# A fused convolution and hard-swish feed-forward kernel: one PSUM tile per output round, a plain first block, weight rounding in two steps

**Chip, cores, metric.** One core of one Trainium2 chip. The metric is the device time of one execution in microseconds (us), the median of several runs.

## The reference

```python
# attention part: causal depthwise convolution of 7 taps, softmax weights per head
w = softmax(weight)                                  # (8 heads, 7)
y[b,s,d] = sum_k w[head(d), k] * x_pad[b, s+k, d]    # x: (8, 4096, 192) fp32
# feed-forward part on the 32768 rows of y
h = y @ w_in                                         # (32768, 192) x (192, 2048)
g = h * clip(h + 3, 0, 6) / 6
out = g @ w_out                                      # (32768, 2048) x (2048, 192)
```

The feed-forward weights arrive as 64-bit floats and are rounded to fp32 on the chip, by integer and fp32 operations on their two halves. Everything else is fp32.

## The kernel before

It works on 32 blocks of 1024 rows. A block has an **h phase** (16 units: six fp32 matmuls, two row tiles side by side, then a Relu on ScalarE and the product g on VectorE) and an **out phase**. The out phase uses Strassen's seven products of half-size matrices in place of eight; they run four side by side in column tiles of 32, in five full rounds and one short one. The sums S1 to S4 of g are made on VectorE.

```python
ps = ctx.enter_context(tc.tile_pool(name="ps", bufs=4, space=bass.MemoryType.PSUM))

def banks():
    return ps.tile([P, 2, N], F32, name="banks")     # two halves, meant as one PSUM bank each; 4 such tiles

def out_phase(i, conv):
    ba, bb, bc = banks(), banks(), banks()
    b = [t[:, k] for t in (ba, bb, bc) for k in range(2)]     # six rounds, three tiles
    def three(k, n, n4, q4):                                  # one full round into b[k]
        side_by_side(*[out_mm(b[k], q, n, q, every) for q in range(NQ)],
                     out_mm(b[k], NQ, n4, q4, every))
    ...
    three(0, 1, 2, 0)
    nc.scalar.copy(out=p1[:], in_=b[0][m])
    piece(p2, 0, b[0], NQ)                                    # also a ScalarE copy
    three(1, 5, 2, 1)
    piece(p2, 1, b[1], NQ)
    for u in conv:                                            # 7 taps of the next block's y
        u()
    three(2, 7, 2, 2)
    ...
```

In block 0 the weights are rounded between the matmuls. One unit (1/8 of `w_in` or of `w_out`) is a chain over three engines:

```python
def to_f32(dst, st):
    low, high = st[:, :, 0], st[:, :, 1]
    nc.scalar.mul(rest, low, 2.0**-52)
    nc.vector.tensor_scalar(scale, high, 0x7FF00000, op0=bitwise_and)
    nc.gpsimd.tensor_scalar(scale, scale, (1023-127) << 20, 0.0, subtract, max)   # L142
    nc.gpsimd.tensor_scalar(scale, scale, 255 << 20, 8.0, min, mult)              # L146
    nc.vector.tensor_scalar(top, high, 0xFFFFF, 0x100000, bitwise_and, bitwise_or)
    nc.vector.scalar_tensor_tensor(sig, top, 2.0**-20, rest, mult, add)
    nc.vector.scalar_tensor_tensor(scale, high, 0x80000000, scale, bitwise_and, bitwise_or)
    nc.gpsimd.tensor_tensor(dst, sig, scale, mult)                                # L161
...
for p in range(NP):                       # NP = 8
    if i == 0:
        ... load two units ahead ...
        if p + 1 < NP: w_in_unit(p + 1)   # rounding, then two swap copies by DMA
    h_unit(i, p); h_unit(i, NP + p)
    if p % 2: s_unit(p - 1)
if i == 0:
    for j in range(NP): w_out_unit(j)     # all of w_out, after the h phase of block 0
out_phase(i, conv_units(i + 1))
```

(Operand names shortened, cuts marked with dots.)

## Time and profile before

| | before |
|---|---|
| median (range) | 2746.17 us (2746.01 to 2746.58, 3 runs) |
| span of the profiled run | 2742.7 us |
| TensorE / VectorE / ScalarE / GpSimd busy | 92 / 72 / 26 / 3% |
| mean granted clock of TensorE | 0.983 |
| block 1 begins | 203.5 us |
| period of blocks 1 to 31 | 81.65 us |

The names of lines in the profile of before: L240 h matmuls, L271 out matmuls, L245 Relu, L246 g, L258 sums, L295 and L319 ScalarE copies of a round, L300 VectorE adds, L211 taps. "banks<-y,w_in" reads "writes tile banks from y and w_in"; each fp32 matmul appears as two records.

### The profile page before, as it was taken

The numbers are of one execution on the slowest core, as the hardware profiler recorded it, in microseconds if no ns is written. First come the engines' busy times: TensorE is split into PE (matmuls) and PEld (weight loads), VectorE is DVE, ScalarE is ACT, GpSimd is POOL, SyncE is SP. The second block draws the span as 40 slices with busy tenths as digits, with TensorE's granted clock in tenths as the row PEclk, the third lists the DMA queues.
The fourth block names the chain that finished last, engine by engine and source line by source line (L and its number), as shares of the span: only waits on it lengthen the run. The fifth ranks groups of instructions, "written<-read, shape, count | busy, mean of one in ns | idle before, by whom it ended". The sixth has DMA issues, their size and how long they took to land.

```text
span 2742.7 us, 37945 instructions
## 1 busy us (share of the span) xinstructions
PE 2530.7 (92%) x16896; PEld 933.7 (34%) x16896; DVE 1969.1 (72%) x1775; ACT 710.2 (26%) x754; POOL 81.6 (3%) x84
## 2 busy tenths in 40 slices
PE   5469999999999999999999999999999999999998
PEld 2113333333333333333333333333333333333332
DVE  5547867777867777877777877777786777786775
ACT  2102322222322222332222332222232222232221
POOL 2440000000000000000000000000000000000000
PEclk9679999999999999999999999999999999999999
DMA  3100111100111100111110011110011110011100
GB/s 78 49 21 18 21 24 24 24 10 18 21 24 24 24 13 15 20 24 24 24 24 7 19 23 24 24 24 10 18 21 24 24 24 10 18 21 24 24 13 12
DMA packets 223156, 60.91 MB, mean 22 GB/s; under 512 B 204560, under 2 KB 210704, under 8 KB 222992
## 3 DMA queue, kind: packets, MB, share of 16 engines
q1 hardware_dynamic: 217344, 52.19, 10.3%
q10 hardware_dynamic: 5648, 6.30, 0.9%
q8 instruction: 132, 2.16, 0.3%
q14 instruction: 32, 0.26, 0.0%
HBM read 31.72 MB, written 25.17 MB: 21 GB/s over the span
## 4 chain that ended last, share of the span: by engine, by line
PE 91%; ACT 3%; DVE 3%; POOL 2%; issue 1%; DMA 0%; ACTq 0%; DVEq 0%
PE banks L240 48%; PE banks L271 43%; ACT c L295 2%; DVE c L300 1%; POOL scale L146 1%; POOL scale L142 1%; ACT c L319 1%; POOL w_out L173 0%; DVE y L211 0%; DVE s L258 0%; POOL w_out L161 0%; DVE scale L157 0%; DVE g L246 0%; DMA stage<-in_moe_w_in_dram 0%; DVE g L258 0%
## 5 line engine op out<-in xcount | busy, mean ns | idle before, releaser
L240 PE MATMUL banks<-y,w_in 64*128 64x512 f32 x6144 | 1345.2, 594 | 47.9 <-DVE y L211 26.4
L271 PE MATMUL banks<-g,w_out 128*32 128x512 f32 x6144 | 1188.6, 598 | 91.4 <-POOL w_out L161 46.0
L240 PEld LDWEIGHTS banks<-y,w_in 64*128 64x128 f32 x6144 | 597.8, 188 | 794.8 <-issue 750.3
L245 ACT ACTIVATE r<-banks,half 128x1024 f32<-128x1024 f32 x512 | 570.5, 1114 | 822.2 <-PE banks L240 613.6
L246 DVE SCALAR_TENSOR_TENSOR g<-r,banks 128x1024 f32<-128x1024 f32 x512 | 615.7, 1218 | 201.4 <-ACT r L245 190.1
L271 PE MATMUL banks<-s,w_out 128*32 128x512 f32 x4608 | 673.4, 594 | 64.6 <-ACT c L295 64.6
L271 PEld LDWEIGHTS banks<-g,w_out 128*32 128x32 f32 x6144 | 306.6, 110 | 459.2 <-issue 302.3
L300 DVE TENSOR_TENSOR c<-c,banks 96x512 f32<-96x512 f32 (+1 forms) x256 | 172.5, 684 | 377.5 <-ACT c L295 373.1
L271 PEld LDWEIGHTS banks<-s,w_out 128*32 128x32 f32 x4608 | 183.5, 110 | 546.0 <-issue 413.5
L295 ACT COPY c<-banks 32x512 f32<-32x512 f32 x192 | 111.1, 579 | 952.8 <-PE banks L271 952.4
L211 DVE SCALAR_TENSOR_TENSOR y<-x,c_sb,y 128x1536 f32<-128x1536 f32 x192 | 349.3, 1819 | 6.8
L258 DVE TENSOR_TENSOR g<-g 128x1024 f32<-128x1024 f32 x128 | 156.9, 1226 | 4.4
L258 DVE TENSOR_TENSOR s<-g 128x1024 f32<-128x1024 f32 x128 | 156.9, 1226 | 4.4
L258 DVE TENSOR_TENSOR s<-g,s 128x1024 f32<-128x1024 f32 x128 | 156.8, 1225 | 4.4
L258 DVE TENSOR_TENSOR s<-s,g 128x1024 f32<-128x1024 f32 x128 | 155.9, 1218 | 0.0
L300 DVE TENSOR_TENSOR c<-c,c 96x512 f32<-96x512 f32 x64 | 44.0, 687 | 107.2 <-ACT c L295 106.1
L305 DVE STREAM_TRANSPOSE xt<-c 96x512 f32<-96x512 f32 x128 | 90.6, 708 | 4.4
L319 ACT COPY c<-banks 96x512 f32<-96x512 f32 x32 | 18.6, 582 | 203.6 <-PE banks L271 203.6
L207 DVE TENSOR_SCALAR y<-x,c_sb 128x1536 f32<-128x1536 f32 x32 | 57.8, 1805 | 0.0
L157 DVE SCALAR_TENSOR_TENSOR scale<-stage,scale 128x384 uint32<-128x384 uint32 x16 | 8.9, 559 | 48.7 <-POOL scale L146 48.7
L142 POOL TENSOR_SCALAR scale<-scale 128x384 uint32<-128x384 uint32 x16 | 24.4, 1524 | 76.3 <-DVE scale L138 76.3
L146 POOL TENSOR_SCALAR scale<-scale 128x384 uint32<-128x384 uint32 x16 | 24.0, 1503 | 1.3
(21 smaller groups left out, 72.2 us busy)
## 6 DMA issues: line engine op xcount, KB each, us to landing
out_dram<-xt SPq DMA_DIRECT2D x384, 64.0 KB, 2.0
x<-in_x_dram SPq DMA_DIRECT2D x56, 388.5 KB, 5.7
x<-in_x_dram SPq DMA_DIRECT2D x8, 384.0 KB, 4.8
stage<-in_moe_w_in_dram ACTq DMA_DIRECT2D x16, 192.0 KB, 3.5
stage<-in_moe_w_out_dram ACTq DMA_DIRECT2D x8, 384.0 KB, 3.1
w_in<-w_in SPq DMA_DIRECT2D x16, 96.0 KB, 2.2
w_sb<-in_weight_dram ACTq DMA_DIRECT2D x2, 1.8 KB
```

Of the source, the lines that this page charges most:

```text
L142: nc.gpsimd.tensor_scalar(out=scale[:], in0=scale[:], scalar1=float((1023 - 127) << 20), scalar2=0.0, op0=ALU.subtract, op1=ALU.max,)
L146: nc.gpsimd.tensor_scalar(out=scale[:], in0=scale[:], scalar1=float(255 << 20), scalar2=8.0, op0=ALU.min, op1=ALU.mult,)
L207: nc.vector.tensor_scalar(out=y[:], in0=x[:, :, 0:N], scalar1=c, scalar2=None, op0=ALU.mult)
L211: nc.vector.scalar_tensor_tensor(out=y[:], in0=x[:, :, k : k + N], scalar=c, in1=y[:], op0=ALU.mult, op1=ALU.add,)
L240: nc.tensor.matmul(out=h[:, k], lhsT=w_in[r, slots[k], s, :], rhs=y[r, s, :], start=(s == 0), stop=(s == K3 - 1),)
L245: nc.scalar.activation(r6[:], h[:], ACT.Relu, bias=half[:], scale=1.0 / 6.0)
L246: nc.vector.scalar_tensor_tensor(out=g[:, c % NP, c // NP], in0=r6[:], scalar=1.0, in1=h[:], op0=ALU.min, op1=ALU.mult,)
L258: nc.vector.tensor_tensor(out=o[:, r], in0=x[:, r], in1=y[:, r], op=op)
L271: lambda p=p: nc.tensor.matmul(out=bank[j * QS : (j + 1) * QS], lhsT=w_out[:, p, w, cols], rhs=x[:, p], start=(p == ks[0]), stop=(p == ks[ ...
L295: nc.scalar.copy(out=dst[q * QS : (q + 1) * QS], in_=src[j * QS : (j + 1) * QS])
L300: nc.vector.tensor_tensor(out=out, in0=x, in1=y, op=op)
L305: nc.vector.transpose(out=xt[:], in_=c)
```

## The change

The intent: (1) every out round takes a tile of its own, so that TensorE never waits for the evacuation of a neighbour; for that the order of the products becomes 1, 4, a short 2, 7, 6, 3, and S2 and S4 are made late in wide instructions. (2) Block 0 needs no sums: it multiplies plain g, eight half products. (3) Rounding of weights is cut in a first and a second step, one unit begun ahead; the clamp moves from GpSimd to ScalarE. (4) All loads are issued up front; the first convolution goes in thirds, so that the first four h units can begin with the first third of y.

```diff
-    stg = ... bufs=3;  cnv = ... bufs=2
+    stg = ... bufs=2 * NP;  cnv = ... bufs=3
...
+        def first(self):
+            nc.vector.tensor_scalar(scale, high, 0x7FF00000, bitwise_and)
+            nc.vector.tensor_scalar(top, high, 0xFFFFF, 0x100000, bitwise_and, bitwise_or)
+            nc.scalar.activation(over, scale, Relu, bias=bias_e[:, 0:1], scale=-1.0)
+            nc.scalar.activation(scale, over, Relu, bias=bias_e[:, 1:2], scale=-8.0)
+            nc.scalar.mul(rest, low, 2.0**-52)
+        def second(self):
+            nc.vector.scalar_tensor_tensor(scale, high, 0x80000000, scale, ...)
+            nc.vector.scalar_tensor_tensor(sig, top, 2.0**-20, rest, mult, add)
+            nc.gpsimd.tensor_tensor(dst, sig, scale, mult)
+            self.then()                                   # w_in: the two swap copies
...
+    w_in_st = [load_w_in(nc.scalar if j < 2 else nc.sync, j) for j in range(NP)]
+    w_out_st = [load_w_out(nc.sync, j) for j in range(NP)]
...
-        ba, bb, bc = banks(), banks(), banks()
-        b = [t[:, k] for t in (ba, bb, bc) for k in range(2)]
+        def three(n, n4, q4):
+            bank = banks()[:, 0]
...
+    def out_direct(i, work):                              # block 0: plain products
+        parts = [(k, q) for k in range(G) for q in range(G * NQ)]
+        for r in range(0, len(parts), 4):
+            bank = banks()[:, 0]
+            ... four column tiles x 16 matmuls, transpose from PSUM, store ...
...
+        begin(); begin(); ... next(ended).second(); next(ended).second()
+        conv0 = conv_units(0, [slice(s, s + 1) for s in range(K3)])
+        for s in range(K3):
+            for u in conv0[s * KC : (s + 1) * KC]: u()
+            advance(1) if s else begin()
+        early = [(c, banks()) for p in range(2) for c in (p, NP + p)]
+        for s in range(K3):
+            for c, h in early: h_mm(0, c, h, s)
+        for n, (c, h) in enumerate(early):
+            h_out(c, h)                                   # Relu, g
+            if n: advance(1)                              # begin a unit, end one
+        for p in range(2, NP):
+            h_unit(0, p); advance(1)
+            h_unit(0, NP + p)
+            if p < 5: advance(1)
+        out_direct(0, conv_units(1, [slice(0, K3)]))
```

## The prediction

> **What bounds the kernel now.** I read the page first (busy shares, the 40 slices), then the chain that ended last over one block in the middle, then the waits of TensorE in two stretches (0 to 204 us and from 200 us on), then the chain and the windows of the start.
>
> From the page: TensorE is the busy engine, but its first slices are poor, at a low granted clock.
>
> ```profile
> PE 2530.7 (92%) x16896; PEld 933.7 (34%) x16896; DVE 1969.1 (72%) x1775; ACT 710.2 (26%) x754; POOL 81.6 (3%) x84
> ...
> PE   5469999999999999999999999999999999999998
> ...
> PEclk9679999999999999999999999999999999999999
> ```
>
> A slice is 68.6 us. So the kernel has two regimes: a start of some 200 us, and 31 equal blocks. One block of the second regime, from the chain (start us, length us, what):
>
> ```profile
> 203.61 41.40 PE banks L240 x192
> 245.01 7.08 PE banks L271 x64
> ...
> 252.11 0.58 ACT c L319
> ...
> 252.71 0.59 ACT c L295
> ...
> 253.34 13.98 PE banks L271 x128
> ...
> 267.35 0.59 ACT c L295
> ...
> 267.98 13.98 PE banks L271 x128
> ...
> 281.99 0.59 ACT c L295
> ...
> 282.60 0.69 DVE c L300
> ...
> 283.33 1.92 PE banks L271 x16
> 285.26 1.05 PE banks L240 x3
> ```
>
> The period is 285.26 - 203.61 = 81.65 us, and in it TensorE stops three times for an evacuation: after out rounds 1, 3 and 5, never after 2 and 4. Rounds 1 and 2 write the two halves of one tile (`ba`), 3 and 4 of `bb`, 5 and 6 of `bc`: the second half waits until the readers of the first half are through, although it writes other addresses. The waits of TensorE from 200 us on say the same in total (us, times, longest):
>
> ```profile
> PE banks L271 <- ACT c L295: 62.5, 62, 1.3
> PE banks L271 <- DVE c L300: 45.4, 32, 1.4
> ```
>
> That is 107.9 us over 31 blocks, 3.48 us in each. The same question for 0 to 204 us gives the start's own waits; its two largest:
>
> ```profile
> PE banks L271 <- POOL w_out L161: 46.0, 8, 12.6
> PE banks L240 <- DVE y L211: 26.4, 1, 26.4
> ```
>
> TensorE waits for the rounding of the weights: the chain of the start has two GpSimd steps of 1.5 us per unit (L142, L146), 16 units one after the other, the last eight of them in out round 1 of block 0 (matmuls at 120.03, 126.75, 133.48 ..., every 6.7 us). Block 1 begins at 203.5 us.
>
> **What the Trainium skill says.** (1) "Perfetto Trace Analysis", section "Matmuls": independent matmul groups should rotate through different PSUM banks, so that the evacuation of one lies beside the matmuls of the next. The trace agrees: the three waits stand exactly where two rounds share a tile. (2) "TensorE: Matmul & The Clock Gate", section "Wait — 56ns, not 53.3ns?": a warm pass of N columns starts every N / 2.4 GHz + about 2.5 ns, so 512 columns take 215.8 ns, and at half clock twice the column time. Here a fp32 pair (two row tiles) or quad (four column tiles) starts every 0.431 us, two such passes; the first ones after the start stand 0.85 us apart, from 26.44 to 29.87 us. (3) "DMA: Bandwidth & Descriptors", section "Queues, rings and completion order": each issuing engine has one ring per DMA engine, consumed in ring order. No run here shows a long backlog: the swap copies of `w_in` land in 2.2 us (median) because little stands before them. (4) "PSUM — Partial Sum Buffer", section "Engine vs sequencer instructions": ScalarE and VectorE are strict FIFO; in the trace, too, their instructions run in program order.
>
> **Part 1: one tile per out round.** A block has 96 pairs in the h phase (192 records / 2) and 84 half-passes in quads: 10,752 out records / 32 blocks / 4. That is 180 starts; at 0.4315 us (41.41 us / 96 from first h start to first out start) they take 77.7 us. The new order has just as many: five rounds of 128 records and a short one of 16. So each block can lose 81.65 - 77.7 = 3.95 us: the 3.48 us of waits and three drains of the array of about 0.17 us that then lie under the next round. Times 31: 122 us.
>
> Does a new wait come? With four tiles, each request waits for the readers of the one four before it. Let T be the end of the h phase. VectorE: last g at T+2.4; S1, S3 of the last pair until T+4.9; the four wide sums S2, S4 (2048 columns, estimated 2.3 us from 1.22 us per 1024) until T+14.1; four taps of 1.85 us until T+21.5; the short round's adds and one store until T+25; three taps until T+30.6; then the adds of rounds 7 and 6. TensorE's rounds end at T+6.9, 13.8, 15.5, 22.4, 29.3, 36.2. S2 is needed at T+22.4, S4 at T+29.3, y at T+36.2 (slack 5.6 us). The next block's first four h units take the tiles of the short round (free at T+25), of 7 and of 6 (T+33), and of 3 (T+38, needed at T+44). Nothing waits. VectorE in total per block: 16 g (19.5) + 16 half sums (19.0) + taps (12.9) + 10 adds and 4 transposes (9.7) = 61 of 77.7 us; not the bound.
>
> **Part 2: block 0 with plain products.** It removes the S sums (16 x 1.22 = 19.6 us of VectorE) from the start and costs TensorE 12 outputs x 16 steps / 4 side by side x 2 = 96 starts instead of 84: 41.4 us instead of 36.2, so +5.2 us.
>
> **Part 3: rounding in two steps, clamp on ScalarE.** GpSimd loses 2 x 1.5 us per unit and keeps the product (1.0 us); VectorE keeps 0.35 + 0.35 + 0.56 + 0.61, with issue 1.95 us; ScalarE goes from one instruction of 0.55 us to three, 1.65 us. One unit is begun ahead of the one that is ended. But the order is strict: g of unit n, then the bit operation of a new unit on VectorE, then three ScalarE instructions, and only behind these the Relu of h unit n+1, on which the next g waits. One round trip: 1.22 + 0.35 + 0.08 + 1.75 + 1.11 + 0.04 = 4.5 us, against 2.58 us of TensorE for an h unit. Eleven such trips lie in block 0: 50 us.
>
> **Part 4: conv by thirds and loads up front.** Stage 0 lands at 9.3 us as now. VectorE: bit operations, c_sb, both second steps until about 14.3, then three thirds of 7 x 0.67 us with a rounding between: 19, 24.5, 31.3 us. TensorE could start at 19 us. But the swap copies, without which no h unit is complete, go to the SP ring behind the loads that were issued before them. All loads are 7.1 MB; from 2 to 10 us the queues moved 198 GB/s, with some 225 at the plateau, so they end at 2.2 + 31.5 = about 33.5 us, and the first swap lands then. So thirds gain nothing. Four early units: 24 pairs with a cold beginning; the first is through at 43.3, its Relu at 44.4. g0, g1 until 47; ten round trips and g11 until about 92.5; this frees the tile of the last h unit, which ends at 96 to 97 (clock 0.8 as now in that stretch). Then 41.4 us of direct rounds, with the last rounding, the last g (102 us) and conv 1 (13 us) beside them: **block 1 begins at about 137 us**, against 203.5. If the swaps land early, at about 128.
>
> **The sum.** 136 (between the two, nearer the first) + 31 x 77.7 = 2408.7, + tail. The tail is now 2742.7 - (203.5 + 31 x 81.65) = 8.1 us: a copy, three small adds, an add, a transpose (4.1 us), stores. New: three adds and two transposes (3.6 us), so 7.6. Span 2552. The runs stand 3.5 us above the span of the profile now (2746.2 against 2742.7): **2556 us**, ratio 0.931.
>
> **The rivals.** (a) A new wait in each block, because y, S2 or a tile comes late: VectorE has 5.6 us of slack ahead of the h phase; 1 us of wait in each block makes +31 us, 2587. For it: VectorE is in order and its queue is full from T to T+33. Against: 61 of 77.7 us. (b) The start gains what its author wants: no backlog, TensorE from 19 us on, ScalarE and VectorE not in each other's way (3.2 us per unit, the VectorE sum): block 1 at 115, 2535 us. (c) The start gains little: loads slower than now, half clock through block 0 (5.15 us per h unit): block 1 at 155, 2575 us. (d) The waits within a tile were only the cover of another limit, such as the weight loads of the column tiles: then 81.65 stays, and the time is 2675. Against: after rounds 2 and 4 nothing waits now, and starts stay 0.43 us apart.
>
> **Range and chances.** The 31 blocks are sure to about +0.5 us each (+15 us, hardly anything below), the start to about -18 and +15. So 2536 to 2580. Faster by over 2% (under 2691) even where (a) or (c) comes true: 0.98.
>
> **What will show it.** The period of a block, first h matmul to first h matmul, should be 77.7 us, with no wait of TensorE on an evacuation; a period of 78.5 or more means (a), 81.6 means (d). The first h matmul at 33 us shows the backlog, at 19 us none. Gaps between successive g of 4.5 us show the round trip, 3.2 us rival (b). The end of block 0 should stand at 128 to 140 us, and GpSimd should be busy for about 16 + 7 us. I am wrong if the block period misses 77.7 by over 0.5 us or block 1 begins outside 115 to 155.

## The result, and the profile after

| | before | after |
|---|---|---|
| median (range) | 2746.09 us (2744.26 to 2746.58, 4 runs) | 2548.68 us (2548.14 to 2549.26, 4 runs) |
| span of the profiled run | 2742.7 us | 2547.2 us |
| block 1 begins | 203.5 us | 133.6 us |
| period of blocks 1 to 31 | 81.65 us | 77.59 us |
| from the last block's end to the end | 8.1 us | 8.3 us |
| mean granted clock | 0.983 | 0.999 |

The ratio is 0.9282, 95% interval 0.9266 to 0.9298. A ratio here is the mean time of one kernel's fast runs over that of the other's in the same rounds, so not quite the ratio of the medians.

The page of after, busy time and two of the rows of 40 slices:

```profile
PE 2495.4 (98%) x16944; PEld 945.9 (37%) x16944; DVE 1923.2 (76%) x1640; ACT 740.9 (29%) x810; POOL 28.6 (1%) x24
...
PE   4899999999999999999999999999999999999998
...
PEclk9999999999999999999999999999999999999999
```

The poor first slices have shrunk from three to two, and the clock is full almost everywhere. (Before 36.9 us the trace of after holds no clock record, which the page counts as full clock; the weight loads of successive pairs stand 0.85 us apart there from 33.1 to 36.5 us, against 0.43 later.) Line numbers have moved: L254 h matmuls, L281 out matmuls, L262 Relu, L263 g, L231 taps of y, L184 and L185 the swap copies, L158, L161 and L164 the rounding on ScalarE, L148 the first bit operation, L347 and L364 (L365 in one run) ScalarE copies of a round. The chain over one block in the middle (start us, length us, what):

```profile
873.30 36.19 PE banks L281 x336
909.49 41.40 PE banks L254 x192
950.89 9.13 PE banks L281 x81
```

Where before had three copies and an add between pieces of out rounds, the out phase is one piece of 336 records, and the period is 950.89 - 873.30 = 77.59 us. All of TensorE's waits in the whole run (us, times, longest) are now these three, and all lie before 92 us:

```profile
PE banks L254 <- DVE y L231: 23.7, 1, 23.7
PE banks L254 <- DVE g L263: 13.3, 9, 1.6
PE banks L254 <- DMA w_in<-w_in: 6.4, 1, 6.4
```

From the chain of the start:

```profile
17.33 6.57 DMA stage<-in_moe_w_out_dram
...
23.98 8.09 DMA w_in<-w_in
...
32.12 10.39 PE banks L254 x35
...
92.27 41.34 PE banks L281 x384
```

The first h matmuls that matter start at 32.12 us, when the first swap copy has landed; the plain out phase of block 0 runs from 92.27 to 133.60 us. Between, the chain goes round a loop over two engines, once per h unit:

```profile
57.81 0.04 DVE g L263
...
58.95 0.36 DVE scale L148
...
59.34 0.63 ACT over L158
...
60.05 0.62 ACT scale L161
...
60.66 0.45 ACT rest L164
...
61.12 1.01 ACT r L262
...
62.15 0.06 DVE g L263
```

From g to g it takes 62.15 - 57.81 = 4.34 us, and the Relu (ACT r, L262) stands behind three rounding instructions, which wait for VectorE's bit operation, which waits in VectorE's order for the g before.

So the saving of 195.5 us in span is 31 x 4.06 = 125.9 us in the blocks and 69.9 us in the start, minus 0.2 at the end.

### The profile page after: what moved, and what is told of

The parts are those of the page before. It is cut to its first block, busy times and chain, and to the rows that moved or that the text cites. A ratio compares the mean times of both kernels' runs of the same rounds, so it can differ in the third digit from the quotient of the medians.

```text
span 2547.2 us, 37923 instructions
## 1 busy us (share of the span) xinstructions
PE 2495.4 (98%) x16944; PEld 945.9 (37%) x16944; DVE 1923.2 (76%) x1640; ACT 740.9 (29%) x810; POOL 28.6 (1%) x24
## 4 chain that ended last, share of the span: by engine, by line
PE 97%; ACT 1%; DMA 1%; issue 1%; DVE 0%; ACTq 0%; SPq 0%; DVEq 0%
PE banks L254 51%; PE banks L281 46%; ACT r L262 0%; DMA stage<-in_moe_w_in_dram 0%; DMA w_in<-w_in 0%; DMA stage<-in_moe_w_out_dram 0%; ACT over L158 0%; ACT rest L164 0%; ACT scale L161 0%; DVE g L263 0%; DVE scale L148 0%; SPq L112 0%; DVE c L352 0%; ACTq L112 0%; ACTq L85 0%
## 5 line engine op out<-in xcount | busy, mean ns | idle before, releaser
L254 PE MATMUL banks<-y,w_in 64*128 64x512 f32 x6144 | 1334.4, 591 | 43.4 <-DVE y L231 23.7
L263 DVE SCALAR_TENSOR_TENSOR g<-r,banks 128x1024 f32<-128x1024 f32 x512 | 623.3, 1218 | 428.6 <-ACT r L262 428.6
L254 PEld LDWEIGHTS banks<-y,w_in 64*128 64x128 f32 x6144 | 598.1, 187 | 779.2 <-issue 751.7
L262 ACT ACTIVATE r<-banks,half 128x1024 f32<-128x1024 f32 x512 | 569.9, 1114 | 789.5 <-PE banks L254 723.8
L281 PE MATMUL banks<-g,w_out 128*32 128x512 f32 x6336 | 739.4, 593 | 0.0
L281 PE MATMUL banks<-s,w_out 128*32 128x512 f32 x4464 | 643.6, 592 | 0.0
L281 PEld LDWEIGHTS banks<-g,w_out 128*32 128x32 f32 x6336 | 215.4, 110 | 516.1 <-issue 491.5
L231 DVE SCALAR_TENSOR_TENSOR y<-x,c_sb,y 128x1536 f32<-128x1536 f32 (+1 forms) x204 | 356.1, 1745 | 6.1
L281 PEld LDWEIGHTS banks<-s,w_out 128*32 128x32 f32 x4464 | 183.5, 110 | 296.8 <-issue 296.5
L347 ACT COPY c<-banks 32x512 f32<-32x512 f32 x186 | 107.7, 579 | 601.6 <-PE banks L281 600.9
L352 DVE TENSOR_TENSOR c<-c,banks 32x512 f32<-32x512 f32 (+1 forms) x186 | 127.4, 685 | 138.9 <-ACT c L347 133.8
L409 DVE TENSOR_TENSOR s<-g,s 128x2048 f32<-128x2048 f32 x62 | 139.1, 2284 | 0.0
L409 DVE TENSOR_TENSOR s<-s,g 128x2048 f32<-128x2048 f32 x62 | 139.0, 2284 | 0.0
L352 DVE TENSOR_TENSOR c<-c,c 96x512 f32<-96x512 f32 x124 | 83.9, 677 | 3.2
L364 ACT COPY c<-banks 96x512 f32<-96x512 f32 x31 | 18.0, 582 | 184.0 <-PE banks L281 184.0
L368 ACT COPY c<-banks 96x512 f32<-96x512 f32 x31 | 18.0, 582 | 176.4 <-PE banks L281 176.4
L227 DVE TENSOR_SCALAR y<-x,c_sb 128x1536 f32<-128x1536 f32 (+1 forms) x34 | 57.4, 1689 | 0.0
L158 ACT ACTIVATE over<-scale,bias_e 128x384 f32<-128x384 uint32 x16 | 9.9, 617 | 41.0 <-DVE scale L148 41.0
```

The costliest lines, as they stand in the source:

```text
L227: nc.vector.tensor_scalar(out=y[:, part], in0=x[:, part, 0:N], scalar1=c, scalar2=None, op0=ALU.mult)
L231: nc.vector.scalar_tensor_tensor(out=y[:, part], in0=x[:, part, k : k + N], scalar=c, in1=y[:, part], op0=ALU.mult, op1=ALU.add,)
L254: nc.tensor.matmul(out=h[:, k], lhsT=w_in[r, slot, s, :], rhs=y[r, s, :], start=(s == 0), stop=(s == K3 - 1),)
L262: nc.scalar.activation(r6[:], h[:], ACT.Relu, bias=half[:], scale=1.0 / 6.0)
L263: nc.vector.scalar_tensor_tensor(out=g[:, c % NP, c // NP], in0=r6[:], scalar=1.0, in1=h[:], op0=ALU.min, op1=ALU.mult,)
L281: lambda p=p: nc.tensor.matmul(out=bank[j * QS : (j + 1) * QS], lhsT=w_out[:, p, w, cols], rhs=x[:, p], start=(first and p == ps_[0]), sto ...
```

## The experiments

Every experiment changes one of the two kernels in one place, except where it says so, and gave correct results. Those sent together shared the runs of the kernel before on their chip (medians 2744.8 to 2745.7 us). The twelve answer two questions: is the shared tile alone the cause in the 31 blocks, and what paces block 0? Where block 1 begins is read from one profiled run of each kernel. Five kernels with the same start (the change, and its variants that differ only from block 1 on) have it at 132.1 to 133.6 us, so a difference of under 1.5 us there says nothing.

### The kernel before, with one tile per round and nothing else

```diff
-        ba, bb, bc = banks(), banks(), banks()
-        b = [t[:, k] for t in (ba, bb, bc) for k in range(2)]
+        b = []
         def three(k, n, n4, q4):
+            b.append(banks()[:, 0])
...
         n = NP // 4
+        b.append(banks()[:, 0])          # the short round
```

> The kernel before, with the one edit that each of its six out rounds takes a tile of its own; order of the products, start and sums untouched. My theory (the waits come from two rounds sharing one tile, and nothing else in the change is needed to lose them): period of a block 77.6 us instead of 81.65, no wait of TensorE on an evacuation from 210 us on, block 1 still begun at about 202 us, so 2746 - 31 x 4.05 = about 2620 us. Rival (the new order of the products and the wide late sums are needed too, because the old order holds tiles too long): a wait stays, period 78.5 to 80, 2650 to 2700 us.

Measured: 2615.06 us, ratio 0.9525 (0.9512 to 0.9538). Its chain in the middle:

```profile
938.20 36.19 PE banks L271 x336
974.39 41.40 PE banks L240 x192
1015.79 36.19 PE banks L271 x336
```

The period is 1015.79 - 938.20 = 77.59 us, that of the whole change; no wait of TensorE is left after block 0. Block 1 began at 198.5 us and not at about 202: block 0 loses its own three waits too (3.5 us in before), and TensorE is back at full clock earlier there (pairs 0.43 us apart from 170.0 us on, in before from 173.4). So 131 of the 197 us come from a few lines; the new order of the products, and the wide late sums, take nothing further off a block.

### The change, with two rounds sharing a tile again

```diff
+        two = banks()
-        b = three(1, 2, 0)
+        b = three(1, 2, 0, two[:, 0])
...
-        b = three(4, 2, 1)
+        b = three(4, 2, 1, two[:, 1])
```

> The changed kernel, with only its first two long out rounds in the two halves (two different banks) of one tile again. My theory (the wait is for the readers of the same tile): one wait per block is back, two copies of 0.6 us plus about 0.2 us of drain, 1.5 us; period 79.1 us, 2549 + 47 = about 2595 us. Rival (what bound the rounds before was something other than the shared tile): period stays 77.6, 2549 us.

Measured: 2595.65 us, ratio 0.9454 (0.9442 to 0.9467), 47 us above the change. The chain has the old picture back, once per block:

```profile
965.38 7.08 PE banks L281 x64
...
972.48 0.58 ACT c L365
...
973.07 0.59 ACT c L347
...
973.71 29.39 PE banks L281 x272
```

The matmuls of the second round go to the other half of the tile than the one the copies read, and still start only when both copies are through. The period is 1044.50 - 965.38 = 79.12 us. It is the tile that is waited for, not the addresses: the framework that orders the instructions treats the two halves as one.

### The change, with block 1 plain too

```diff
-                if p % 2:
+                if p % 2 and i > 1:
                     s_sums(...)
-            out_strassen(i, ...)
+            (out_strassen if i > 1 else out_direct)(i, ...)
```

> The changed kernel, with block 1 also done by products of plain g (no sums). Measures the price of the plain form in TensorE starts where nothing else is short: 12 starts of 0.43 us more, so block 1 lasts 82.8 us instead of 77.6, and the kernel 2554 us, +5.2 us. Rival (the plain form costs less because its streams need no extra round, or more because a single tile per round is evacuated late): block 1 at 77.6, or over 84 us.

Measured: 2553.63 us, ratio 0.93 (0.9287 to 0.9313). Block 1 ran from 133.26 to 216.00 us, 82.74 us, 5.15 more than a Strassen block. That is the price of the plain form in TensorE time, as worked out.

### The change, with S2 and S4 made twice; and with S2 made twice

```diff
-        s_sums(every, (2, 4), 4)
+        s_sums(every, (2, 4, 2, 4), 4)      # second run: (2, 4, 2)
```

> The changed kernel, with its four wide sums S2 and S4 of each block computed twice (same values, 9.0 us more of VectorE per block). Tests how much slack VectorE has before y of the next block is needed: the trace of the change shows the last tap at T+30.1 us and the next h phase at T+36.2, 6.1 us. My theory: TensorE now waits 9.0 - 6.1 = 2.9 us for y in 30 blocks, period 80.5, about 2636 us. Rival (VectorE is in truth the bound already, every us counts): +9 us per block, 2820 us; other rival (far from it): no change, 2549 us.

Measured: 2679.2 us, ratio 0.9759 (0.9746 to 0.9773): 131 us above the change where I expected 87. The waits of TensorE from 200 us on:

```profile
PE banks L254 <- DVE y L231: 84.5, 30, 2.8
```

The wait is 84.5 / 30 = 2.82 us, as expected from 9.0 - 6.1. The rest is in the h phase behind it, which lasts 42.93 us and not 41.40. The weight loads of TensorE show why (each pair of h matmuls has two):

```profile
950.91 0.37 PEld L254 LDWEIGHTS banks<-y,w_in 64*128 64x128 f32 x2 [0.48 <-issue]
951.77 0.37 PEld L254 LDWEIGHTS banks<-y,w_in 64*128 64x128 f32 x2 [0.49 <-issue]
...
953.19 0.20 PEld L254 LDWEIGHTS banks<-y,w_in 64*128 64x128 f32 x2 [0.23 <-issue]
953.62 0.20 PEld L254 LDWEIGHTS banks<-y,w_in 64*128 64x128 f32 x2 [0.23 <-issue]
```

Pairs stand 0.86 us apart at first and 0.43 later: TensorE comes back from the wait at half clock, for some 3 us, which costs 1.53 us. Together 2.82 + 1.53 = 4.35 us per block, times 30 is 130.5. By the clock records of the packed trace each stretch at half clock lasts 3.413 us, and they come every 81.92 us in all 30 blocks, which is 24 times that length; so the 1.53 us may depend on how the block fits this grid. No other length of wait was run.

> The changed kernel with S2 alone computed twice, 4.5 us more of VectorE per block instead of the 9.0 us of the run before. Theory (VectorE has 6.1 us of slack before y is needed, and below it nothing is paid): 2549 us, period 77.6, clock 1.0. In the run with 9.0 us the wait of 2.8 us per block also brought half clock for some 3.3 us after it (+1.5 us). Rival (slack is not the measure, and VectorE's work always costs something): +1 us or more per block, 2580 us.

Measured: 2548.89 us, ratio 0.9285 (0.927 to 0.9299), period 77.59: 4.5 us more work of VectorE per block cost nothing. So VectorE's slack lies between 4.5 and 9.0 us, and the trace's 6.1 gave the wait to a tenth. Rival (a) of the prediction was not far away: in this kernel some 6 us of further VectorE work per block are free by the trace (4.5 by this run), and at 2.8 us beyond that a microsecond cost more than a microsecond. Shorter waits may not: those of up to 1.4 us in before left the clock full.

### The start: swap copies ahead of the loads of w_out

```diff
-    w_out_st = [load_w_out(nc.sync, j) for j in range(NP)]
+    w_out_st = [stage() for j in range(NP)]
...
         next(ended).second()
         next(ended).second()
+        for j in range(NP):
+            load_w_out(nc.sync, j)
         conv0 = ...
```

> The changed kernel, with the eight loads of w_out issued from the SP queue only after the swap copies of the first two w_in units. My theory (the first swap is late because it is issued and served behind those loads): the swap lands before 23 us instead of 32.1, TensorE runs each third of the h products as soon as its third of y is there (23.7, 30, 36.3 us), the first g comes at 38.5 instead of 43.7 us, block 1 begins at 128.4 instead of 133.6, the kernel takes about 2543.5 us (-5). Rival (the loads or the cold clock only move the wait to a later place in block 0): block 1 stays at 133 us, 2549 us.

The ground for it in the trace of after, the SP queue in order of time:

```profile
17.33 6.02 SPq L120 DMA_DIRECT2D stage<-in_moe_w_out_dram  x8
...
23.98 0.53 SPq L184 DMA_DIRECT2D w_in<-w_in  x1
```

The first swap (L184) was ready when GpSimd ended its product at 17.36 us, was issued only behind the eight loads at 23.98, and landed 8.09 us later, where 2.2 us is the median in the kernel before.

Measured: 2545.75 us, ratio 0.9272 (0.9259 to 0.9284), 2.9 us less than the change. TensorE, in order of time:

```profile
23.75 9.42 PE L254 MATMUL banks<-y,w_in 64*128 64x512 f32 x32 [23.75 <-DVE y L231]
36.53 13.72 PE L254 MATMUL banks<-y,w_in 64*128 64x512 f32 x50 [3.36 <-DVE y L231]
```

The wait for the swap is gone, and TensorE starts with each third of y as intended. It gained 3.3 us at the beginning of block 1 (130.31 us; 1.7 us against the earliest of the five kernels with the old start) and not 5.2: after the new wait of 3.4 us for the last third TensorE restarted at half clock, so the first g came at 39.8 and not at 38.5 us, 3.9 us earlier than in the change.

### The start: Relu ahead of the rounding

```diff
-        for n, (c, h) in enumerate(early):
-            h_out(c, h)
-            if n: advance(1)
-        for p in range(2, NP): ...
+        for n, (c, _) in enumerate(todo):               # all 16 h units
+            ahead = (products of unit n+1, its Relu)    # issued first
+            h_out(c, h, r6)                             # g of unit n
+            h, r6 = ahead
+            if 0 < n < 10 or n in (10, 12, 14): advance(1)
```

> The changed kernel, with the products and the Relu of the next h unit issued ahead of the rounding steps in block 0 (the Relu stands before the three rounding instructions in ScalarE's order, no longer behind them). My theory (block 0 is paced by a round trip VectorE-ScalarE-VectorE of 4.33 us per h unit because both are in order): distance of successive g falls to about 3.0 us, the last h product ends 12 us earlier, block 1 begins at about 121 us, 2536 us. Rival (VectorE's or ScalarE's sum of work is the bound, or the loads of w_in): distances stay above 4 us, 2549 us.

Measured: 2532.53 us, ratio 0.9224 (0.9211 to 0.9237), 16.2 us less than the change.

```profile
31.93 43.32 PE banks L254 x190
75.25 41.34 PE banks L284 x384
```

From 31.93 us on TensorE does not wait once; the distance of successive g is 2.61 us (59.52 to 62.12 us and the like), against 2.58 us for an h unit of TensorE. Block 1 begins at 116.59 us, 17 us earlier. My 3.0 us per unit was too long: g, the bit operations and the second step follow each other on VectorE without a gap, overlap a little, and take these 2.61 us. So VectorE is as full there as TensorE, and a shorter distance would need less work on both.

### Both edits

The two diffs above together.

> Both edits, swaps first and Relu ahead. If the two causes lie one behind the other in block 0 the gains add up: -5 and -12.5 us, block 1 at about 116 us, 2531 us. If they hide each other: no better than the better of the two, 2536 us.

Measured: 2529.67 us, ratio 0.9213 (0.92 to 0.9225), block 1 at 113.78 us. The gains add up: 3.3 and 17.0 apart, 19.8 together.

### The first convolution in one piece

```diff
-        conv0 = conv_units(0, [slice(s, s + 1) for s in range(K3)])
+        conv0 = conv_units(0, [slice(0, K3)])      # the other two rounds of the loop: only advance
```

> The changed kernel, with the first convolution in one piece instead of three. My theory (the thirds bring nothing, because the first swap lands at 32.1 us and y in one piece is there at about 31 us): block 1 begins at 133.6 us +- 1.5, 2549 us. Rival (thirds matter as the change means them to): TensorE starts later and block 1 begins 4 us or more later, 2553 us or more.

Measured: 2548.65 us, ratio 0.9282 (0.9269 to 0.9295), block 1 at 133.11 us. The thirds bring nothing as long as the swap comes at 32 us; y in one piece was complete at 30.63 us.

### The clamp back on GpSimd

```diff
-            nc.scalar.activation(over, scale, Relu, bias=bias_e[:, 0:1], scale=-1.0)
-            nc.scalar.activation(scale, over, Relu, bias=bias_e[:, 1:2], scale=-8.0)
+            nc.gpsimd.tensor_scalar(scale, scale, (1023-127) << 20, 0.0, subtract, max)
+            nc.gpsimd.tensor_scalar(scale, scale, 255 << 20, 8.0, min, mult)
```

> The changed kernel with the clamp of the exponent back on GpSimd (two instructions of 1.5 us, as in the kernel before), everything else of the change kept: two-step units, plain block 0, loads up front. Theory (with two-step units the clamp is off the chain wherever it is; what paces block 0 is who stands before the Relu in ScalarE's order): the round trip over ScalarE shrinks to one short instruction, and GpSimd's own work of 1.54 + 1.50 + 1.0 us and gaps, 4.1 us per unit, takes its place; distance of successive g 4.0 to 4.3 us, block 1 begins within 3 us of 133.6, 2549 us +- 3. Rival (the move of the clamp to ScalarE is what makes the start short, as the change means it): distance back to 6 us or more, 11 x 2 us longer, 2570 us or more.

Measured: 2549.64 us, ratio 0.9287 (0.9275 to 0.93), 1 us above the change; block 1 at 133.75 us. The time is as expected, the distance less so: 4.03 us for the first units, then 4.81. In the longer ones `sig` on VectorE takes 1.35 us instead of 0.55 and the product on GpSimd 1.36 instead of 1.00, each beside the other. The loop lost on GpSimd what it gained on ScalarE.

### Units in one step

```diff
-            advance(1) if s else begin()
+            if s:
+                advance(1)
```

> The changed kernel with no unit begun ahead: each unit's first step is followed at once by its own second step (the edit drops the one extra first step after the first third of the convolution). Theory (block 0 is paced by the Relu that stands behind the rounding instructions in ScalarE's order; VectorE's second step of 1.0 us fits beside that Relu of 1.1 us whether it belongs to this unit or the one before): distance of successive g stays at about 4.4 us, block 1 begins within 3 us of 133.6, 2549 to 2552 us. Rival (the two steps are what takes ScalarE's time off VectorE's path): distance 5.5 us or more, 11 x 1.2 us later, 2561 us or more.

Measured: 2547.99 us, ratio 0.9284 (0.9271 to 0.9297), distance of successive g 4.33 us, block 1 at 132.20 us. Beginning a unit ahead brings nothing either: VectorE's second step fits beside the Relu for which the next g waits anyway.

### Both edits, and the first third ahead of the second unit

```diff
         begin()
-        begin()
         c_sb = e_sb * sm
+        for u in conv0[:KC]: u()           # first third of y
+        begin()
         next(ended).second(); next(ended).second()
...                                         # with the two edits above
```

> Swaps first and Relu ahead, and besides the first third of the first convolution moved ahead of the second weight unit's first step, into the time in which VectorE idled for that unit's load (2.8 us) . After the two edits TensorE waits only for y (its last wait ends at 36.3 us, when the third of the thirds is done). Theory: y is the next bound, the last third comes 3 to 4 us earlier, the kernel takes about 2526 us, 3.5 us less than with the two edits. Rival (the first swap, which waits for the rounding that now stands behind the third, becomes the bound): no gain, 2529.7 us.

Measured: 2527.41 us, ratio 0.9207 (0.9196 to 0.9219), block 1 at 111.98 us, 1.8 us earlier than with the two edits: half of what I expected. The last third of y was there at 34.34 and not at 36.34 us, and about 1 us after the restart, though the wait had been only 1.73 us, TensorE fell to half clock again (pairs 0.85 us apart from 35.6 to 38.2 us). By its median this is the fastest version run, 21.3 us below the change; one of its six runs, 2529.55 us, lies among those of the two edits.

## Why the prediction was right or wrong

The predicted time was 2556 us, the measured 2548.7, inside the range. By its steps:

- **One tile per round.** Right, in cause and size. Predicted period 77.7 us, measured 77.59; 31 blocks saved 125.9 us and not 122. The first experiment shows that nothing else in the change is needed for it, the second that one shared tile brings one wait back. Rival (d), that the waits covered another limit, is refuted by both; its 2675 us should have been 2678 by the prediction's own terms. The page "Perfetto Trace Analysis" of the Trainium skill, section "Matmuls", which the prediction names, speaks of PSUM banks; here the two rounds already stood in different halves of a tile, meant as different banks, and waited all the same, so its "the trace agrees" holds for the tiles and not for the banks.
- **No new wait.** Right. The last tap ended at T+30.1 us (expected 30.6), and doubling S2 and S4 showed the edge of the slack. I had said that 1 us of wait in each block would make +31 us; a long wait costs more, as the half clock behind it adds half as much again.
- **Block 0 plain.** The +5.2 us of TensorE was measured as 5.15 in block 1. That leaving out the sums in block 0 pays for it was only argued: no run has Strassen in block 0 with the new start. GpSimd was busy for 28.6 us and not 16 + 7: the four wide sums of `w_out` (L195) took 11.8 us beside the taps of y, of which one took up to 3.27 us there and not 1.82.
- **The round trip.** Right: predicted 4.5 us, measured 4.33, and putting the Relu first takes it away. So the change's own idea, the clamp on ScalarE and units in two steps, was worth nothing by itself here (two experiments, each taking one of them back: +1.0 and -0.7 us).
- **Loads up front.** Right that the first swap waits behind them: predicted 33.5 us, measured 32.1. The mechanism was incomplete, and the number is near partly by luck. I took 225 GB/s for all loads; from 8 to 23 us, with those of x and `w_in` under way (64 partitions each, runs of 1 KB for `w_in`), the queues moved 207 to 228 GB/s, but from 23 to 30 us, with those of `w_out` (128 partitions, runs of 1.5 KB), some 370. With 220 and 370 my sum would have ended at about 29 us (an estimate); which of the differences sets the rate no run shows. What I left out made up for it: I had only the ring in mind, but the SP queue itself was also held up, and issued the swap 6.6 us after it was ready (17.36 to 23.98). By the semaphores in the packed trace, each DMA waits for the landing of the one eight before it; for the first swap that was the first load of `w_out` (issued at 17.33, landed 6.57 us later). I had placed the first third of y at 19 us; it came at 23.6, because the second `w_in` unit landed at 14.1 us and not near 11, with more loads beside it.
- **The beginning of block 1.** 137 us at the late swap, 136 in the sum; measured 133.6. The mis-sized term is the end of the last h unit, 96 to 97 us by a clock of 0.8 and 4.5 us per trip; it ended at 92.27 us with the clock at 1.00 and 4.33 us per trip.
- **The ends.** The tail was set at 7.6 and is 8.3 us: the last add waits for ScalarE's copy out of the same tile, which I had put beside it. The runs stand 1.5 us above the profiled span where I took 3.5 us; the profiled run of before, at 2744.56, was itself faster than the median I compared its span with.

So the error of some 7 us is 2.4 (block 1) + 3.4 (31 x 0.11) + 2.0 (offset) - 0.7 (tail).

**What stays open.** The start gave 65 us from the first experiment (block 1 at 198.5) to the change (133.6). What is left for it is that the eight `w_out` units no longer stand one after the other behind the h phase (every 6.7 us, 46 us of waits in before) but between its units, that their four differences (L173, 1.8 us of each 6.7) are no longer needed in block 0, that block 0 makes no sums, and that loads come early. The trace fits the first best; no run separates the four. The thirds, the clamp's engine and the two steps, each taken back alone, are excluded within 2 us.

## What to carry to other kernels

Two accumulation groups that follow each other should not share a tile in a framework like this one, even if they lie in different halves of it: the second here waited for every reader of the first, and giving each its own tile cost nothing here and made 66% of the gain. When several engines work strictly in order, look for the one instruction that TensorE needs next and put it ahead of the work that only has to be done sometime; moving part of that work to another engine, or cutting it up, changed the time here by 1 us at most, and putting the needed instruction first by 16. A transfer that is small but needed first should be issued ahead of the bulk loads of the same queue (2.9 us here).

## What the Trainium skill lacked or had wrong

- "TensorE: Matmul & The Clock Gate", section "What's actually happening", has half clock after at least one idle window of about 3.4 us. Here the clock fell with no idle window of that length: after waits of 2.82 us (h phases of 42.93 us instead of 41.40) and once about a wait of 1.73 us. By the clock records of the packed traces, in the 3.4 us before the fall TensorE had been busy for some 1.0 us in the first case and 1.7 us in the second (with the profile's modelled ends of matmuls). The three waits of 0.7 to 1.4 us per block in the kernel before, and those of 1.4 to 1.6 us in block 0 of the change, never made it fall.
- No page says that a DMA here also waits for an older one: in this program each waits for the landing of the one eight before it, of either queue, because eight semaphores go round. SP issued its third load of `w_in` at 7.61 us, when the first load of ScalarE's queue had landed at 7.59; twelve loads of 192 KB (about 0.6 us each when free) took it 14.1 us, 6.7 us of it in such waits.
